# A sequence transform on 96-row runs, with both mirrors on partitions of their own, in a fused 2D-FFT and maxout kernel

## The chip, the cores and the metric

The kernel runs on one core of one Trainium2 chip. The metric is the time on the device in microseconds (us), the median of several runs. "Before" is the kernel as it stood, "after" the kernel with the change.

## What is computed

```python
X = np.fft.fft(x, axis=1)              # x: 8 x 3072 x 256, float32
X = np.fft.fft(X, axis=2).real         # over the sequence, then over the features
t = X.reshape(8 * 3072, 256)
h = np.maximum(np.maximum(t @ w1, t @ w2), t @ w3)      # w1, w2, w3: 256 x 768
out = h @ w_out                        # w_out: 768 x 256, out: 24576 x 256, float32
```

The matmuls run in bf16 with float32 sums. The transform over the features is a 256 x 256 matrix, so it is multiplied into w1, w2, w3 and w_out once, at the start; the tables and the products are made on the chip. What is left for each batch is the transform over the 3072 rows. x is real, so row 3072 - k of the result is row k with the mirror image of its features: the kernel computes the 1536 rows of one half (tE, the part even in k, and tO, the odd part) and forms both halves' hidden layers from them, with sums and differences of the same products.

## The kernel before

The kernel is written for a planner that keeps the order of the program: each engine gets its instructions in the order in which the Python code issues them, and waits are put in by data dependence. So the order of the lines is the order of each engine's queue, and a place in a queue is a decision of the author. A DMA is issued by an engine (SP, ACT or POOL) and takes a place in that engine's queue too.

**x comes in** as 24 x 128: row n = 128 a + bb, with `load_rows` (L100). A batch is cut into four chunks of 32 bb; each chunk is four DMAs, one for each group of 64 features, so that partition (group, a) holds rows of 64 float32, 256 bytes each. Later batches go through SP's queue into `xs` (four buffers); batch 0 is split over all three queues. `turn_chunk` (L118) is the POOL copy that casts a chunk to bf16 and turns it, so that for each feature `dl` the 128 bb lie side by side. It may be given an instruction that it has to follow ("folds first").

**Stage one**, `Mix.s` (L337, L339): 64 matmuls per batch, one for each `dl`, with x (96 x 128) as the loaded weights and `m24blk` (96 columns: 24-point cosines and sines for four feature groups) moving. Thirteen PSUM groups are evicted by ACT to `ub`.

**The folds**, `Mix.fold` (L350 to L373): DVE adds and subtracts features and their mirror images, from `ub` into `zE` and `zO`, in bf16, some in descending order.

**Stage two**, `Mix.k` (L387 to L399): 44 matmuls of 128 columns and 6 of 64, with zE or zO as weights and the tables `cos_t`, `sin_t`, `nsin_t` moving; ACT evicts the six groups to `tE` and `tO`. `end` does the one row in the middle of the half (`t_mid`, three matmuls of one column).

**The two layers.** A batch is three blocks of 512 rows, a block six groups `jc` of 128 hidden columns: 18 **units** a batch. A unit is `unit_plus` (L415, L416: four matmuls of 512 columns into `pse2` and `pse3`, which have two buffers each), `unit_out` for the rows k (ACT takes ReLU of one at L429, DVE the maximum with the other at L430: `hp`), then `finish` of the unit before: `unit_minus` (L423, two matmuls of 512 columns into the same PSUM, with `gD`, the difference to the rows 3072 - k) and a second `unit_out` (`hm`). Then `l2_some(10)` issues ten steps of the second layer of the block before: `l2_block`, four slots of 128 rows each with 12 matmuls of 256 columns (L439), the linear part (L455, L463), DVE's sum `ot` (L468), one direct store on SP (L483, rows k, 24 apart) and one indirect store on POOL (L473, rows 3072 - k). The maximum of three is taken as relu(difference) and max because w1's product is taken off the other two and given back by the linear part.

**The plan.** After a unit's second layer, pieces for the next batch are issued from a table, filled by `at(batch, unit, piece)` (L611): `s0` to `s12`, the folds `fA0` to `fC1`, `kE0` to `kO2`, `end` (lists `ahead`, `ahead0`, and the first unit `begin`, 5 from batch 2 on), the casts of the batch after that (each behind the last fold) and the loads of the one after. So the sequence transform of a batch is spread over the units of the batch before it.

**The start.** Before any unit, the tables (L215 to L232), batch 0's x, the weights (POOL's queue, both halves of w1, w2 and w3 early, L159 to L168), twelve matmuls without use for the clock (L565), stage one, the folds and kE0, kO0 of batch 0, and the products `gE`, `gO`, `gD` for the first half of the hidden columns (`product`, `keep_product`, L268, L280, L281; gD is POOL's). The second half (`prep_first`) and the second layer's product `gw` (`prep_second`) are placed by `prep_some`: the first of them ahead of the first unit.

**The end.** The last block's second layer is `l2_last` (L486): direct stores only, all on SP's queue but the first of the last slot, which is on ACT's (L519). The middle rows of all batches are done together in `l2_mid`.

Of the kernel before, what the change touches and what calls it, by code (L numbers as in the profile page):

```python
# [9 lines left out]
FP32 = mybir.dt.float32  # L10
# [9 lines left out]
def _reduce(nc, w, v, q, period, rnd, neg):  # L20

    shape = list(v.shape)
    for c in (rnd, neg):
        assert c.shape[0] == shape[0]
    wide = [shape[0], v.free_size()]
    nc.vector.scalar_tensor_tensor(out=q, in0=v, scalar=1.0 / period,
                                   in1=rnd.to_broadcast(wide), op0=ALU.mult, op1=ALU.add)
    nc.vector.scalar_tensor_tensor(out=q, in0=q, scalar=-ROUND,
                                   in1=neg.to_broadcast(wide), op0=ALU.add, op1=ALU.mult)
    nc.vector.tensor_tensor(out=w, in0=v, in1=q, op=ALU.add)  # L30


@with_exitstack
def kernel(
# [18 lines left out]

    DLS = ((20, 25), (25, 30), (30, 35), (35, 40), (40, 45),
           (15, 20), (45, 50), (10, 15), (50, 55),
           (5, 10), (55, 60), (60, 64), (0, 5))
# [7 lines left out]
    xs_pool = ctx.enter_context(tc.tile_pool(name="xs", bufs=4))  # L64
    x0_pool = ctx.enter_context(tc.tile_pool(name="x0", bufs=2))
    u_pool = ctx.enter_context(tc.tile_pool(name="ubuf", bufs=1))
    z_pool = ctx.enter_context(tc.tile_pool(name="zbuf", bufs=1))
    t_pool = ctx.enter_context(tc.tile_pool(name="tbuf", bufs=2))

    m24blk = consts.tile([96, 96], BF16, tag="m24blk")  # L70
# [4 lines left out]
    cos_t = consts.tile([128, 13 * 128], BF16, tag="cos_t")  # L75
    sin_t = consts.tile([128, 13 * 128], BF16, tag="sin_t")
    nsin_t = consts.tile([128, 13 * 128], BF16, tag="nsin_t")
# [14 lines left out]
    zO = consts.tile([128, 26 * 128], BF16, tag="zO")  # L92

    def x_rows(b):
        return x[b].rearrange("(a bb) (g dl) -> g a bb dl", bb=128, g=4)

    def load_rows(eng, dst, b, r0, r1, after=None):
        xr = x_rows(b)
        for g in range(4):
            ld = eng.dma_start(out=dst[g * 24:(g + 1) * 24], in_=xr[g, :, r0:r1, :])  # L100
            if after is not None:
                tc.add_manual_dep(ld.ins, after.ins.name, AFTER, reason="weights first")

    def load_chunk(b, ch, after=None):
        xs = xs_pool.tile([96, 32 * 64], FP32, name="xs", tag="xs")
        load_rows(nc.sync, xs.rearrange("p (bb dl) -> p bb dl", dl=64), b,
                  ch * 32, ch * 32 + 32, after)
        return xs

    raw = {}  # L110
    turned = {}

    def turn_chunk(b, ch, after=None):

        if ch == 0:
            x0 = x0_pool.tile([96, 64 * 128], BF16, name="x0", tag="x0")
            turned[b] = x0.rearrange("p (dl bb) -> p dl bb", bb=128)
        cast = nc.gpsimd.tensor_copy(turned[b][:, :, ch * 32:(ch + 1) * 32],  # L118
                                     raw.pop((b, ch)).rearrange("p (bb dl) -> p dl bb", dl=64))
        if after is not None:  # L120
            tc.add_manual_dep(cast.ins, after.ins.name, AFTER, reason="folds first")
# [10 lines left out]
    HEAD = 80  # L132
    staged = []
    for (r0, eng) in ((80, nc.sync), (96, nc.scalar), (112, nc.sync)):
        xs = xs_pool.tile([96, 32 * 64], FP32, name="xs", tag="xs")
        load_rows(eng, xs[:, 0:16 * 64].rearrange("p (bb dl) -> p bb dl", dl=64), 0, r0, r0 + 16)
        staged.append((r0, xs))
# [178 lines left out]
    class Mix:  # L316
# [25 lines left out]
        def fold(self, k, which):  # L342
# [10 lines left out]
            if k < 2:  # L353
                return
# [377 lines left out]
```

## Time and profile before

| what | value |
|---|---|
| median of 3 runs | 432.57 us (431.87 to 433.15) |
| span of the profiled execution | 431.8 us |
| mean granted clock of TensorE | 0.996 |
| PE busy | 404.8 us, 94% of the span |
| DVE, ACT, POOL busy | 307.7 us, 272.8 us, 238.0 us |
| moved by DMA | 51.58 MB in 127,333 packets, 109,233 of them under 512 bytes |
| SP's queue (q1, hardware) | 44.8% of 16 DMA engines' span |
| ACT's queue (q10, hardware) | 0.8% |
| POOL's queue (q0, software) | 17.8% |

The profile is one execution. PE is the matmul engine, PEld its weight loads (beside the matmuls), DVE the vector engine, ACT the scalar engine, POOL GpSimd, SP the queue that only issues DMAs. Busy is the time inside instructions, added up; "x" counts them. Matmuls overlap, so a busy PE says little of whether it is at its peak: for that the starts of matmuls one after the other have to be compared. A row of a timeline has the start, the length, the engine, line, operation, the tiles (out<-in), shapes, and how many were drawn together; brackets name what ended the wait ahead of it. In a row of a group, the numbers behind the bar are busy us, mean ns of one, idle us ahead of them and what ended it. A row of a source line has smallest, median and largest length in ns and the first and last time.

### The profile page before, as it was taken

To read this page: it belongs to the slowest core of one execution; us is meant where nothing else is said; L and a number is where in the kernel's file an instruction comes from. 1 tells how busy PE (TensorE), PEld (TensorE's weight loads), DVE (VectorE), ACT (ScalarE), POOL (GpSimd) and SP (SyncE) were. 2 spreads that over 40 slices of the span, in tenths; PEclk is the share of its full clock that TensorE was granted. 3 is DMA by queue.
4 is the path that set the end of the run, shared out by engine and by line. 5 is a ranking of instruction groups with operands and counts; after the bars stand their busy time and mean duration, and the time that the engine had idled before them with its cause. 6 is when DMAs were issued, how large, how long until landed. Compare 5 with 4: busy or idle time off the path is not lost.

```text
span 431.8 us, 9121 instructions
## 1 busy us (share of the span) xinstructions
PE 404.8 (94%) x3196; PEld 271.1 (63%) x3252; DVE 307.7 (71%) x611; ACT 272.8 (63%) x512; POOL 238.0 (55%) x256
## 2 busy tenths in 40 slices
PE   0499979999999999999999999999999999999996
PEld 0175656666666666666666666667666666666665
DVE  7766748856886769576876679576876679667673
ACT  3576557666866676657765676757765676754650
POOL 7546762598249823984279624984369623214320
PEclk9989999999999999999999999999999999999999
DMA  9999999559731969159761969158762222111213
GB/s 115 111 160 124 128 139 192 152 113 174 147 107 53 179 131 204 63 99 160 145 145 73 167 127 199 73 97 155 148 141 74 74 63 74 62 56 52 105 66 130
DMA packets 127333, 51.58 MB, mean 119 GB/s; under 512 B 109233, under 2 KB 124344, under 8 KB 127288
## 3 DMA queue, kind: packets, MB, share of 16 engines
q1 hardware_dynamic: 104936, 35.80, 44.8%
q0 software_dynamic: 20624, 14.68, 17.8%
q10 hardware_dynamic: 1728, 0.52, 0.8%
q8 instruction: 25, 0.41, 0.4%
q14 instruction: 20, 0.16, 0.2%
HBM read 28.31 MB, written 25.17 MB: 124 GB/s over the span
## 4 chain that ended last, share of the span: by engine, by line
PE 84%; DVE 5%; ACT 4%; issue 2%; DMA 2%; POOL 1%; SPq 1%; ACTq 0%; DVEq 0%; POOLq 0%
PE po L439 27%; PE pse L415 14%; PE pse L423 13%; PE pse L416 11%; PE ps L337 6%; PE po L463 4%; PE pl L455 2%; DMA xs<-in_x_dram 2%; DVE hm L430 1%; ACT stmp L429 1%; PE warm L565 1%; PE psg L268 1%; PE ps L394 1%; DVE ot L468 1%; POOL x L118 1%
## 5 line engine op out<-in xcount | busy, mean ns | idle before, releaser
L429 ACT ACTIVATE stmp<-pse 128x512 bf16<-128x512 f32 x288 | 167.6, 605 | 57.4 <-PE pse L416 45.5
L473 POOL DMA_INDIRECT out_dram<-ot,rows_m x92 | 101.8, 1107 | 160.5 <-DVE ot L468 144.0
L430 DVE TENSOR_TENSOR hp<-pse,stmp 128x512 bf16<-128x512 f32 x144 | 99.3, 689 | 98.9 <-ACT stmp L429 64.9
L118 POOL CAST x<-xs 96x2048 bf16<-96x2048 f32 x28 | 104.6, 3745 | 11.3 <-DMA xs<-in_x_dram 8.8
L415 PE MATMUL pse<-tE,gE 128*128 128x512 bf16 x280 | 106.1, 379 | 2.2
L430 DVE TENSOR_TENSOR hm<-pse,stmp 128x512 bf16<-128x512 f32 x144 | 98.6, 685 | 6.3 <-ACT stmp L429 6.0
L416 PE MATMUL pse<-tO,gO 128*128 128x512 bf16 x245 | 92.7, 379 | 0.5
L439 PE MATMUL po<-wout_bf,hp 128*128 128x256 bf16 x576 | 86.1, 273 | 0.1
L423 PE MATMUL pse<-tO,gD 128*128 128x512 bf16 x284 | 84.9, 379 | 0.6
L439 PE MATMUL po<-wout_bf,hm 128*128 128x256 bf16 x576 | 78.6, 273 | 0.0
L339 ACT CAST ub<-ps 128x480 bf16<-128x480 f32 (+1 forms) x102 | 51.7, 556 | 37.2 <-PE ps L337 37.2
L439 PEld LDWEIGHTS <-hp 128*128 128x128 bf16 x576 | 56.4, 98 | 26.1
L439 PEld LDWEIGHTS <-hm 128*128 128x128 bf16 x576 | 56.4, 98 | 16.3
L468 DVE TENSOR_TENSOR ot<-po,even 128x512 f32<-128x512 f32 x92 | 62.7, 682 | 0.0
L423 PEld LDWEIGHTS <-gD 128*128 128x128 bf16 x288 | 27.7, 98 | 32.5 <-POOL gD L281 0.5
L416 PEld LDWEIGHTS <-gO 128*128 128x128 bf16 x288 | 28.1, 98 | 19.8 <-issue 1.6
L415 PEld LDWEIGHTS <-gE 128*128 128x128 bf16 x288 | 28.0, 97 | 19.5 <-issue 0.8
L337 PE MATMUL ps<-m24blk,x 96*128 96x96 bf16 x512 | 33.3, 213 | 2.7 <-POOL x L118 1.7
L463 PE MATMUL po<-gw,tO 128*128 128x512 bf16 x91 | 34.5, 379 | 0.0
L337 PEld LDWEIGHTS <-x 96*128 96x128 bf16 x512 | 30.5, 111 | 5.0 <-POOL x L118 2.0
L399 ACT CAST tO<-ps 128x512 bf16<-128x512 f32 x24 | 14.1, 586 | 22.4 <-PE ps L396 14.0
L459 ACT COPY even<-pl 128x512 f32<-128x512 f32 x46 | 27.3, 593 | 0.1
(127 smaller groups left out, 309.1 us busy)
## 6 DMA issues: line engine op xcount, KB each, us to landing
xs<-in_x_dram SPq DMA_DIRECT2D x112, 192.0 KB
out_dram<-ot SPq DMA_DIRECT2D x90, 128.0 KB
out_dram<-ot,rows_m POOLq DMA_INDIRECT x92, 4.4
w_bf<-in_moe_w_dram POOLq DMA_DIRECT2D x6, 192.0 KB, 5.6
out_dram<-ot SPq DMA_DIRECT2D x17, 64.0 KB
xs<-in_x_dram SPq DMA_DIRECT2D x8, 96.0 KB
x<-in_x_dram POOLq DMA_DIRECT2D x8, 96.0 KB, 11.5
xs<-in_x_dram ACTq DMA_DIRECT2D x4, 96.0 KB
```

The lines of the kernel that those rows point to most:

```text
L118: cast = nc.gpsimd.tensor_copy(turned[b][:, :, ch * 32:(ch + 1) * 32], raw.pop((b, ch)).rearrange("p (bb dl) -> p dl bb", dl=64))
L337: nc.tensor.matmul(ps1[:, i * 96:(i + 1) * 96], x0[:, d0 + i, :], m24blk, start=True, stop=True)
L339: evict(out=self.ub[:, d0 * 96:d1 * 96].rearrange("p (c i) -> p c i", i=n), in_=ps1[:, 0:n * 96].rearrange("p (i c) -> p c i", c=96))
L415: nc.tensor.matmul(pse[:, 0:n], gE[i][:, js], te, start=True, stop=False)
L416: nc.tensor.matmul(pse[:, 0:n], gO[i][:, js], to, start=False, stop=True)
L423: nc.tensor.matmul(pse, gD[i][:, js], to, start=False, stop=True, skip_group_check=True)
L429: nc.scalar.activation(out=stmp[:, 0:n], in_=pses[0][:, 0:n], func=AX.Relu)
L430: nc.vector.tensor_tensor(out=dst, in0=src3, in1=stmp[:, 0:n], op=ALU.max)
L439: nc.tensor.matmul(po, hcols(jc), wout_bf[:, jc * 256:(jc + 1) * 256], start=False, stop=(jc == NJC - 1), skip_group_check=True)
L463: nc.tensor.matmul(po, to[:, cp], gw[:, 256:768], start=True, stop=True)
L468: nc.vector.tensor_tensor(out=ot.rearrange("p (h c) -> p h c", h=2), in0=po.rearrange("p (h c) -> p h c", h=2), in1=lin.unsqueeze(1).to_br ...
L473: stored(nc.gpsimd.indirect_dma_start(out, bass.IndirectOffsetOnAxis(ap=rows_m[0:128 - lo, b * 12 + slot: b * 12 + slot + 1], axis=0), ot[ ...
```

## The change

x is now read as 32 runs of 96 rows: row n = 96 a + s, s from 0 to 95. A partition of `xr` holds (feature half m, mirror h, a): 2 x 2 x 32 = 128. With h = 0 it has s = 0 to 48, with h = 1 the same features of rows 96 - s (`load_x`; the rows are read in descending order), each piece 128 features or 512 bytes long. x is read so that each row is fetched once. The turn to bf16 is in two halves: m = 0 in four pieces on POOL (`turn_low`), m = 1, with its features in descending order, in eight pieces on DVE (`turn_high`) and a small copy. The plan has no rule that a POOL piece follows a DVE instruction any more.

Stage one's matmul sums over all 128 partitions, so that it adds both the row's mirror image and the feature's at once: 64 matmuls of 64 columns (`tab1`) and a small one (`tabx`) for each batch; ACT evicts eight groups and a small one to `tb`. In place of the folds, `y` issues four DMAs on ACT's queue, from SBUF to SBUF (64 partitions, two pieces of 2,176 bytes each), which bring the two feature halves and cosine and sine parts together in `yb`; `j` (twice, on DVE, 128 x 2,176, bf16) brings them into the order in which stage two takes them as weights, `yc`. Stage two has one matmul where there were two: 30 of 96 columns, eight of 32 or fewer, and two of one column, with tables `te_tab` and `to_tab` of 1,537 columns.

The rows of a slot are now 32 apart, in two or three stretches (`_runs`): 25 direct stores a batch for 13. At the end two stores are on ACT's queue for one.

The plan: stage one in units 6 to 9 (9 to 12 in batch 0), `y` behind the last piece, `j` in units 11 and 12 (14 and 15), stage two in units 12 to 17. The loads of batch b are in units 0 to 6 of batch b - 2, its turns on POOL and DVE in units 9 to 16 of the same.

The start: ACT issues half of batch 0's loads (eight DMAs) ahead of its own work. The second half of w1, w2 and w3, w_out and batch 1's x wait for the last of the first `y`'s DMAs. Batch 0's turns are on POOL (one), ACT (three) and DVE (four and the small one). There are 24 matmuls for the clock.

```diff
+def _runs(slot):
+
+    g, sub = divmod(slot, 4)
+    q = 5 * g + 1
+    if sub == 0:
+        special = {0: [(0, 32, 0)], 1: [(0, 16, 1024), (16, 32, 16)], 2: [(0, 32, 528)]}[g]
+        return special + [(32, 128, q)]
+    if sub == 1:
+        return [(0, 96, q + 1), (96, 128, q + 2)]
+    if sub == 2:
+        return [(0, 64, q + 2 + 1024), (64, 128, q + 3)]
+    return [(0, 32, q + 3 + 2048), (32, 128, q + 4)]
...
-    def turn_chunk(b, ch, after=None):
...
-        cast = nc.gpsimd.tensor_copy(turned[b][:, :, ch * 32:(ch + 1) * 32],
-                                     raw.pop((b, ch)).rearrange("p (bb dl) -> p dl bb", dl=64))
-        if after is not None:
-            tc.add_manual_dep(cast.ins, after.ins.name, AFTER, reason="folds first")
+
+    def load_x(b, s0, s1, engs, after=None):
+
+        rows = x[b].rearrange("(a s) (m f) -> m a s f", s=96, m=2)
+        for m in range(2):
+            for h in range(2):
+                lo, hi = (s0, s1) if h == 0 else (max(s0, 1), min(s1, 48))
+                src = rows[m]
+                src = src[:, lo:hi, :] if h == 0 else src[:, 97 - hi:97 - lo, :][:, ::-1, :]
+                p0 = 64 * m + 32 * h
+                ld = engs[h].dma_start(out=xr[b % 2][p0:p0 + 32, lo:hi, :], in_=src)
+                if after is not None:
+                    tc.add_manual_dep(ld.ins, after.ins.name, AFTER, reason="others first")
+
+    def turn(b, s0, s1, m, fn, f0=0, f1=128):
+
+        src, dst = xr[b % 2], xt[b % 2]
+        if m == 0:
+            return fn(out=dst[0:64, f0:f1, s0:s1],
+                      in_=src[0:64, s0:s1, f0:f1].rearrange("p s f -> p f s"))
+        return fn(out=dst[64:128, 1:128, s0:s1],
+                  in_=src[64:128, s0:s1, 127:0:-1].rearrange("p s f -> p f s"))
+
+    def turn_first(b, fn):
+
+        return fn(out=xt[b % 2][64:128, 0, 0:NS], in_=xr[b % 2][64:128, :, 0])
...
+    FIRST = ((0, 16), (16, 30), (30, 41), (41, 49))
+    for c, (s0, s1) in enumerate(FIRST):
+        load_x(0, s0, s1, (nc.sync, nc.scalar))
...
+    _reduce(nc, ang_r, ang_r, ang_q, 32.0)
+    nc.scalar.activation(out=ang_q, in_=ang_r, func=AX.Sin, scale=float(2.0 * math.pi / 32.0))
+    nc.vector.tensor_copy(out=tab1[:, 0:32], in_=ang_q[:, 0:32])
+    scal(tab1[:, 32:64], ang_q[:, 0:32], sig, ALU.mult)
+    scal(tabx, ang_q[:, 2 * RI:4 * RI], sgm, ALU.mult)
...
+    scal(kvec, kvec, sidx, ALU.mult, phi, ALU.add)
+    _reduce(nc, kvec, kvec, q, 3072.0)
...
+    turn(0, *FIRST[0], 0, pool)
+    turn(0, *FIRST[0], 1, dve)
+    turn(0, *FIRST[1], 0, act)
+    turn(0, *FIRST[1], 1, dve)
+    nc.scalar.activation(out=te_tab, in_=kvec, func=AX.Sin, scale=step)
...
+    def load_w(jh, after=None):
...
+            if after is not None:
+                tc.add_manual_dep(ld.ins, after.ins.name, AFTER, reason="others first")
+        return ld
+
+    first_half = load_w(0)
+    turn(0, *FIRST[2], 0, act)
+    turn(0, *FIRST[2], 1, dve)
+    nc.scalar.activation(out=q, in_=kvec, func=AX.Abs)
+    turn(0, *FIRST[3], 0, act)
+    turn(0, *FIRST[3], 1, dve)
+    turn_first(0, dve)
...
-        def s(self, k, x0, pool=ps_f, evict=nc.scalar.copy):
...
+        def s(self, k, pool=ps_f, evict=nc.scalar.copy):
             ps1 = pool.tile([128, 512], FP32, name="ps1", tag="ps")
-            for i in range(n):
-                nc.tensor.matmul(ps1[:, i * 96:(i + 1) * 96], x0[:, d0 + i, :], m24blk,
+            for i in range(8):
+                f = 2 * (8 * k + i)
+                nc.tensor.matmul(ps1[:, i * 64:(i + 1) * 64], self.x[:, f:f + 2, :], tab1,
                                  start=True, stop=True)
...
-        def fold(self, k, which):
...
+            evict(out=tbv[:, :, 0:32, 8 * k:8 * k + 8],
+                  in_=ps1.rearrange("p (i e c) -> p e c i", e=2, c=32))
+            if k == 0:
+                psx = pool.tile([128, 512], FP32, name="psx", tag="ps")
+                nc.tensor.matmul(psx[:, 0:2 * RI], self.x[:, 0:2, :], tabx,
+                                 start=True, stop=True)
+                evict(out=tbv[0:64, 1, :, 0], in_=psx[0:64, 0:2 * RI])
+
+        def y(self):
+            for f in range(2):
+                for cs in range(2):
+                    last = nc.scalar.dma_start(out=ybv[cs * 64:cs * 64 + 64, f],
+                                               in_=tbv[f * 64:f * 64 + 64, :,
+                                                       cs * RI:(cs + 1) * RI, :])
+            return last
+
+        def j(self, e, copy=nc.vector.tensor_copy):
+            copy(out=ycv[:, e].rearrange("p r (f m) -> p r f m", f=2),
+                 in_=ybv[:, :, e].rearrange("p f r m -> p r f m"))
 
         def k(self, which, g):
 
-            er, orr = self.zEr, zOr
-            parts = [(r, r * 128, 128) for r in range(4 * g + 1, min(4 * g + 5, 12))]
-            if g == 2:
-                parts += [(0, 0, 64), (12, 12 * 128, 64)]
+            special = {0: [(0, 0, 32)], 1: [(0, 0, 16), (16, 16, 16)], 2: [(16, 0, 32)]}[g]
+            parts = special + [(5 * g + 1 + i, 32 + 96 * i, 96) for i in range(5)]
+            tab = (te_tab, to_tab)[which]
...
+            for (r, c0, wd) in parts:
+                nc.tensor.matmul(ps2[:, c0:c0 + wd], ycv[:, which, (r - 1) % RI, :],
+                                 tab[:, g * 512 + c0:g * 512 + c0 + wd], start=True, stop=True)
...
+            for (p0, p1, k0) in _runs(slot):
+                row = base + k0
+                stored(nc.sync.dma_start(out=out[row: row + 32 * (p1 - p0 - 1) + 1: 32, :],
                                          in_=ot[p0:p1, 0:256]), "direct", ("scattered",))
...
-                stored(eng.dma_start(out=out[row: row + 24 * (p1 - p0 - 1) + 1: 24, :],
+                eng = nc.scalar if sub == 2 and k < 2 else nc.sync
...
-    for _ in range(12):
-        nc.tensor.matmul(warm, cos_t[:, 1536:1664], cos_t[:, 1152:1664], start=True, stop=True)
+    for _ in range(24):
+        nc.tensor.matmul(warm, md_all[:, 0:128], md_all, start=True, stop=True)
...
+    for k in range(8):
+        m.s(k, pool=ps_s, evict=(act, dve)[k % 2])
+    y_first = m.y()
+    nc.scalar.activation(out=to_tab, in_=q, func=AX.Sin, scale=-step, bias=half_pi)
+
     for half in range(2):
-        keep_product(early[half], 0, half, 0, nc.scalar.copy)
+        keep_product(product(0, half, 0, ps_f, "ps"), 0, half, 0, dve)
     for half in range(2):
-        keep_product(product(1, half, 0, ps_s, "ps"), 1, half, 0, nc.scalar.copy)
+        keep_product(product(1, half, 0, ps_s, "ps"), 1, half, 0, dve)
+    for e in range(2):
+        m.j(e)
+    load_w(1, y_first)
+    wld = nc.gpsimd.dma_start(out=wout_bf.rearrange("p (jc c) -> p jc c", jc=NJC),
+                              in_=moe_w_out.rearrange("(jc p) c -> p jc c", jc=NJC))
+    for (s0, s1) in ((0, 13), (13, 25), (25, 37), (37, 49)):
+        load_x(1, s0, s1, (nc.sync, nc.sync), y_first)
...
+    CHUNKS = ((0, 13), (13, 25), (25, 37), (37, 49))
...
+    def turn_low(b, ch):
+        turn(b, *CHUNKS[ch], 0, pool)
+
+    def turn_high(b, k):
+        s0, s1 = CHUNKS[k // 2]
+        mid = s0 + 6
+        turn(b, *((s0, mid), (mid, s1))[k % 2], 1, dve)
+        if k == 7:
+            turn_first(b, dve)
...
-        at(0, (3, 5, 7, 9)[ch], lambda ch=ch: fetch(2, ch))
+        at(0, (3, 5, 6, 7)[ch], lambda ch=ch: turn_low(1, ch))
+        at(0, (8, 10, 12, 14)[ch], lambda ch=ch: fetch(2, ch))
+        at(1, (0, 1, 3, 4)[ch], lambda ch=ch: turn_low(2, ch))
+    for k in range(8):
+        at(0, (3, 4, 5, 5, 6, 6, 7, 8)[k], lambda k=k: turn_high(1, k))
+        at(0, (16, 17, 18, 19, 20, 21, 22, 23)[k], lambda k=k: turn_high(2, k))
+    for b in range(3, B):
+        for ch in range(4):
+            at(b - 2, (0, 2, 4, 6)[ch], lambda b=b, ch=ch: fetch(b, ch))
+            at(b - 2, (9, 11, 13, 15)[ch], lambda b=b, ch=ch: turn_low(b, ch))
+        for k in range(8):
+            at(b - 2, 9 + k, lambda b=b, k=k: turn_high(b, k))
+
+    ahead0 = {9: ("s0", "s1"), 10: ("s2", "s3"), 11: ("s4", "s5"), 12: ("s6", "s7", "y"),
+              14: ("j0",), 15: ("j1", "kE0", "kO0"), 16: ("kE1", "kO1"), 17: ("kE2", "kO2", "end")}
+    ahead = {6: ("s0", "s1"), 7: ("s2", "s3"), 8: ("s4", "s5"), 9: ("s6", "s7", "y"),
+             11: ("j0",), 12: ("j1", "kE0"), 13: ("kO0",), 14: ("kE1",), 15: ("kO1",), 16: ("kE2",),
+             17: ("kO2", "end")}
```

More of the change, by code (lines that the diff above doesn't have):

```diff
@@ L251 @@
     nc.scalar.activation(out=nmd_all, in_=vm, func=AX.Sin, scale=float(-2.0 * math.pi / 256.0))
[L252 to L260 removed]
+    phi = small("phi")
@@ L616, in piece @@
         if what[0] == "s":
[L617 to L619 removed]
+            mm.s(int(what[1:]))
+        elif what[0] == "y":
+            mm.y()
+        elif what[0] == "j":
+            mm.j(int(what[1]))
         elif what[0] == "k":
```

379 lines of the change are left out of this document (127 added, 252 removed).

## The prediction

> **What bounds the kernel now.** I read the page's busy line and chain first, then the table of stretches, one row for each of two whole batches (18 units of 6 long matmuls each; the marks are the same DVE row one batch apart).
>
> ```profile
> PE 404.8 (94%) x3196; PEld 271.1 (63%) x3252; DVE 307.7 (71%) x611; ACT 272.8 (63%) x512; POOL 238.0 (55%) x256
> PE 84%; DVE 5%; ACT 4%; issue 2%; DMA 2%; POOL 1%; SPq 1%; ACTq 0%; DVEq 0%; POOLq 0%
> ```
> ```profile
> core 0: us, PE busy (x) PEld busy (x) DVE busy (x) ACT busy (x) POOL busy (x), PEclk, DMA share, GB/s
> 175.58:223.97 48.39, 48.02 (x389) 32.40 (x394) 35.49 (x72) 32.52 (x63) 29.32 (x29) 1.00 0.66 132
> 320.75:369.14 48.39, 48.01 (x389) 32.44 (x394) 35.55 (x72) 32.52 (x63) 26.05 (x28) 1.00 0.20 67
> ```
> A batch takes 48.39 us at DMA shares of 0.66 and 0.20 alike, so **x loads cost nothing in the middle**: halving their packets can pay only at the start. A busy PE row says little, so I add up start-to-start distances from PE's timeline:
>
> ```profile
> 52.85 0.22 PE L394 MATMUL ps<-nsin_t,zO 128*128 128x128 bf16 x1
> 52.91 0.22 PE L396 MATMUL ps<-cos_t,zO 128*128 128x128 bf16 x1
> ...
> 53.18 0.19 PE L394 MATMUL ps<-nsin_t,zO 128*128 128x64 bf16 x1
> 53.21 0.19 PE L396 MATMUL ps<-cos_t,zO 128*128 128x64 bf16 x1
> ...
> 204.89 0.59 PE L337 MATMUL ps<-m24blk,x 96*128 96x96 bf16 x10
> 205.31 0.81 PE L415 MATMUL pse<-tE,gE 128*128 128x512 bf16 x2
> ```
> So 128 columns take 0.056 us, 64 take 0.030, 96 take 0.042 (0.42 over 10); 512 take 0.216, 256 take 0.109, in the same timeline. A batch: 108 x 0.216 = 23.3 (pse), 12 x 0.216 = 2.6 and 156 x 0.109 = 17.0 (po, pl), 64 x 0.044 = 2.8 (stage one; the last of each ten is a little wider), 44 x 0.056 + 6 x 0.030 + 3 x 0.027 = 2.7 (stage two). Sum 48.4 = the measured 48.39: **PE has no stall in a steady batch**, so what PE is spared comes off, unless ACT or DVE now makes it wait. A unit without extras is 6 x 0.216 + 10 x 0.109 = 2.38 us.
>
> **The change part by part.**
>
> *PE, steady.* Stage one: 65 matmuls of 64 or fewer columns, 65 x 0.030 = 1.95 for 2.8. Stage two: 30 of 96 columns and 10 of 32 or fewer, 30 x 0.042 + 10 x 0.027 = 1.55 for 2.7. Gain 2.0 per batch; batches 1 to 7: **-14.3**; batch 0's later stage two, inside units 2 to 7: **-0.8**. Widths and weight loads all have rows, so I hold this to 2 us.
>
> *ACT, y().* Thirteen evictions (0.56) become eight and a small one: free, ACT had room. But four DMAs now stand in ACT's queue at the end of unit 9, behind the eviction of s7, before unit 10's two ReLUs.
>
> ```profile
> 205.30 1.02 ACT L339 CAST ub<-ps 128x480 bf16<-128x480 f32 x2 [0.81 <-PE ps L337]
> 206.21 1.11 ACT L429 ACTIVATE stmp<-pse 128x512 bf16<-128x512 f32 x2
> ```
> ```profile
> L519 ACTq DMA_DIRECT2D out_dram<-ot x1: 385/385/385, 427.9 to 427.9; - x1
> L100 ACTq DMA_DIRECT2D xs<-in_x_dram x4: 310/456/626, 0.7 to 2.2; - x4
> ```
> An issue on ACT takes 0.31 to 0.63 us; each y DMA has 128 pieces like L519's, so 4 x 0.37 = 1.5. Take 205.31 as the end of s7: the evictions end at 206.3, the issues at 207.8, the two ReLUs at 208.4 and 209.0. The matmuls of unit 11 may overwrite the psum of unit 9 after the second ReLU; PE would be there at 205.31 + 2.38 = 207.7. It waits 1.3 us for ACT, some more for DVE's max. Bounds: 0.7 (issues at 0.31 and an earlier s7) to 2.0; I take 1.4, seven times: **+9.8**. Should an issue also wait for an older DMA on the same semaphore, that comes on top.
>
> *DVE: folds out, turns and j in.* The folds were some 6.6 us a batch. Added: eight turns of 64 partitions, 6,223 elements, and two joins j of 2,176.
>
> ```profile
> L235 DVE CAST x<-xs 96x1024 bf16<-96x1024 f32 x3 | 2.0, 683 | 2.1 <-DMA xs<-in_x_dram 2.1
> L118 POOL CAST x<-xs 96x2048 bf16<-96x2048 f32 x28 | 104.6, 3745 | 11.3 <-DMA xs<-in_x_dram 8.8
> ```
> L235 is the nearest row: 683 - 150 fixed = 0.52 ns an element, though its operands lie in order and the turns' do not; f32 rows with two inputs (L26, 1,092 ns for 896) give 1.04. At 0.52 the turns are 4.4 us, a j 1.28. Units 9 to 16: DVE 8 x 1.63 (hp, hm and two thirds of an ot at 0.61 each) + 4.4 + 2.6 = 20.0 against PE's 20.9. But in units 11 and 12 DVE has 1.63 + 0.55 + 1.28 = 3.5 against PE's 2.4 and 2.6, and PE is only one unit ahead: I take 0.8 us, six times: **+5**. At 1.04 DVE has 25.5 and PE loses 4 a batch (+24 in all); at best 0. The Trainium skill (VectorE: DVE Perf Modes, "The perf-mode tier table") has a bf16 copy within SBUF at four elements a cycle; by that a j would be some 0.7 us, the +5 nearly nothing, and no row here shows it.
>
> j0 also waits for y to land. Its 1.1 MB is issued by 207.8; indirect stores of 128 KB land 4.4 us after issue, loads of 192 KB in 5.6; DVE reaches j0 near 213. I count nothing; late, it would hold every max behind it.
>
> *POOL.* Four casts of 1,664 or 1,536 elements, at 3745 / 2048 ns, are 3.0 and 2.8 us: 11.5 for 15. Off the path. *SP.* 25 direct stores a batch for 13, at 0.38 us, but 16 loads of half the packets; SP has room. At the end two more stores, one issue each: **+0.4**.
>
> *The start.* Before, s(0) begins at 21.7, the first pse at 33.2, and PE waits 1.73 us for a cast at s(1):
>
> ```profile
> 21.69 3.31 PE L337 MATMUL ps<-m24blk,x 96*128 96x96 bf16 x35 [0.54 <-issue]
> 33.20 0.38 PE L415 MATMUL pse<-tE,gE 128*128 128x512 bf16 x1
> 60.04 0.60 PE L337 MATMUL ps<-m24blk,x 96*128 96x96 bf16 x10 [1.73 <-POOL x L118]
> ```
> ```profile
> w_bf<-in_moe_w_dram POOLq DMA_DIRECT2D x6, 192.0 KB, 5.6
> out_dram<-ot,rows_m POOLq DMA_INDIRECT x92, 4.4
> ```
> After: ACT issues eight x loads first, and the last waits for the fourth to land (1.9 MB: 9 to 12 us, bounded by the 115 GB/s of the page's early slices and about twice that for double packets). Only then comes the table load (1.28) and the sine for tab1: 11.4 to 14.2. DVE stands behind it with some 9.7 us of tables (three passes of 1,537 elements at 0.52 and one at 1.04 ns alone are 4.6): 21 to 24. ACT's te_tab, two turns and an Abs, 1.4 us each, follow, beside DVE's turns: s(0) at 28 (26 to 31). Matmuls and evictions 3, four issues 1.5, landing 4: y landed at 36.7. **load_w(1) waits for exactly this**, and PE's queue holds the product of those weights ahead of the first pse: two issues of 0.72, then 5.6, then 0.7: first pse at 43.7, 10.5 later (bounds 6 to 14). The 1.73 wait goes, since x(1) has 30 us until unit 9: **+9**. Without load_w's wait, y, two j and two evictions would still put it near 40.
>
> **Sum** on the profiled execution's 431.8 (the page gives its span alone; the runs' median is 0.8 above): 431.8 - 14.3 - 0.8 + 9.8 + 5 + 0.4 + 9 = 440.9, with 0.8: **441.7**.
>
> **Rivals.**
>
> *Faster.* ACT's issues and j fall into slack and the start costs +5: 432.6 - 15.1 + 0.4 + 5 + 3 = 426; with the start at +9 still 430. For it: ACT is 63% busy, DVE was full for 14 us of folds without stalling PE. Against: ReLUs are strictly behind the issues, and PE runs one unit ahead at most.
>
> *Slower still: DVE and POOL hinder each other.* Before, the casts carry a wait for the folds; now POOL's casts and DVE's turns stand in the same units 9 to 16. The one meeting of such work in the trace:
>
> ```profile
> L281 POOL TENSOR_SCALAR gD<-gO,dif x4: 1232/1268/1653, 30.9 to 42.7; 128x384 bf16<-128x384 bf16 x4
> 30.89 1.65 POOL L281 TENSOR_SCALAR gD<-gO,dif 128x384 bf16<-128x384 bf16 x1 [5.72 <-ACT gO L280]
> ```
> Beside folds it took 0.4 us more than the others, and a fold of 24 elements beside it took 0.57 us against 0.26. If the later one waits for the other's whole instruction: casts fill 11.5 of 21 us, so of ten DVE pieces 5.5 meet one and wait half of 2.9 each, 8 us; less the 2 us or so of slack, 6 a batch for five batches: +30; if half, +15. It decides from about 0.3 us a meeting, the slack in a unit. 456 to 472. The Trainium skill (SBUF — State Buffer, "Who interferes with whom") says just this: a DVE copy in a two-port mode and a GpSimd instruction exclude each other for the whole instruction. The fold that went on beside gD speaks for something milder, but it had another form.
>
> *The wider x rows do not matter.* Then the start alone loses what I gave them: +3, within the forecast.
>
> **How the numbers follow.** Forecast (434 to 455) 0.45; port rival (455 and up) 0.25; faster 0.25; within 0.3% (1.3 us, about what a measurement of this kernel tells from no change) 0.05. The range runs from 426 to 466, with about one in ten beyond each end.
>
> **What would show it.** PE distances of 0.030 and 0.042 us at the new stage lines; a PE wait for ACT in unit 11 of every batch, with ACTq DMA rows ahead of it; first pse near 44; j at 0.6, 1.3 or 2.4 us; DVE turns of one length (0.55 each) or spread up to 3 us (the port rival). The forecast is wrong if a steady batch is below 47.5 us or above 50, or the first pse comes before 39.

## The result and the profile after

The changed kernel takes 543.85 us (median of 4 runs, 542.98 to 545.9), the kernel before 432.79 us beside it: a ratio of 1.258, 95% interval 1.254 to 1.262. I had forecast 441.7, at most 466. The direction was right, the size was not: 111 us instead of 9.

The busy line and the chain of the page after:

```profile
PE 418.1 (77%) x3113; PEld 260.6 (48%) x3168; DVE 401.2 (74%) x542; ACT 268.1 (50%) x474; POOL 230.8 (43%) x246
PE 52%; DVE 19%; issue 11%; DMA 6%; ACT 4%; ACTq 4%; POOL 1%; DVEq 0%; SPq 0%
```

In the chain, issue is time in which the engine waited for nothing that the profile shows, and ACTq is ACT's queue while it issues DMAs. PE held 84% of the chain before and holds 52% now. DVE has 94 us more of busy time, though it lost its folds. Where the time went is a sum over batches. I take the first `hp` row of each batch as its mark:

| | first mark | batch 0 | 1 | 2 | 3 | 4 | 5 | 6 | last mark to end |
|---|---|---|---|---|---|---|---|---|---|
| before | 34.5 | 51.0 | 49.7 | 48.9 | 48.4 | 48.4 | 48.4 | 48.4 | 54.2 |
| after | 54.8 | 66.4 | 69.8 | 60.4 | 61.2 | 59.5 | 60.5 | 52.8 | 55.8 |

The differences are 20.3 for the start, 87.4 for the seven batches, 1.6 for the end: 109.3, the difference of the spans (541.2 - 431.8 = 109.4). So the start is a fifth of the loss. The batches are nearly all of the rest: 11 to 13 us in each of batches 2 to 5, 15 and 20 in batches 0 and 1, 4 in batch 6. Batch 1 holds six of batch 2's turns on DVE beside all of batch 3's, and DVE is busy for 61.4 of its 69.8 us. Two whole batches in the table of stretches (columns as in the prediction: stretch, length, busy of PE, PEld, DVE, ACT, POOL, granted clock, DMA share, GB/s):

```profile
251.38:312.60 61.22, 50.05 (x377) 31.21 (x382) 47.07 (x61) 31.90 (x59) 28.80 (x29) 0.94 0.48 122
312.60:372.10 59.50, 48.95 (x376) 31.00 (x382) 47.04 (x61) 31.85 (x59) 28.83 (x29) 0.97 0.49 126
```

No engine is full (DVE 47 of 60), the DMA engines are half idle, the clock is below 1. That is the look of engines that wait for one another. In the first of the two PE is idle for 10.8 us: 4.2 for ACT's ReLU, 5.8 for DVE, the rest for an eviction of stage one and a little more. PE's timeline in the batch from 251.4 shows for whom:

```profile
272.76 0.63 PE L339 MATMUL ps<-tab,xt 128*128 128x64 bf16 x16
...
282.85 0.58 PE L385 MATMUL pse<-tE,gE 128*128 128x512 bf16 x1 [4.22 <-ACT stmp L399]
283.23 0.63 PE L386 MATMUL pse<-tO,gO 128*128 128x512 bf16 x1
...
291.20 0.41 PE L368 MATMUL ps<-te_tab,yc 128*128 128x32 bf16 x6 [0.54 <-DVE yc L358]
...
292.99 0.38 PE L385 MATMUL pse<-tE,gE 128*128 128x512 bf16 x1 [0.95 <-DVE hm L400]
```

Sixteen stage one matmuls take 0.47 us up to the next start, 0.029 each: that step of the forecast is right. But PE stands 4.22 us for one ReLU of ACT, then runs at about 0.4 us a matmul of 512 columns (0.216 at full clock), and stands for DVE again and again. ACT's timeline at the same place:

```profile
276.05 1.07 ACT L341 CAST tb<-ps 128x512 bf16<-128x512 f32 x2 [0.31 <-PE ps L339]
277.15 4.46 ACTq L352 DMA_DIRECT2D yb<-tb  x4
281.71 1.09 ACT L399 ACTIVATE stmp<-pse 128x512 bf16<-128x512 f32 x2 [4.59 <-DMA yb<-tb]
```

The four issues of `y` take 4.46 us (0.60, 1.25, 0.63 and 1.86), where I had put 1.5. This is the longest `y` of the eight, the others take 2.8 to 3.9 us, and in batches 0 to 6 PE stands 2.6 to 4.2 us for the ReLU behind them. And DVE's turns have two lengths; its rows, and POOL's casts at the same times:

```profile
238.29 3.13 DVE L126 CAST xt<-xr 64x762 bf16<-64x762 f32 x1
...
243.37 1.01 DVE L126 CAST xt<-xr 64x762 bf16<-64x762 f32 x1
...
246.33 2.54 DVE L126 CAST xt<-xr 64x762 bf16<-64x762 f32 x1
...
289.86 1.28 DVE L358 COPY yc<-yb 128x2176 bf16<-128x2176 bf16 x1
```
```profile
237.83 2.87 POOL L124 CAST xt<-xr 64x1536 bf16<-64x1536 f32 x1
...
245.28 2.88 POOL L124 CAST xt<-xr 64x1536 bf16<-64x1536 f32 x1
```

POOL's casts end at 240.70 and 248.16, the two long turns at 241.42 and 248.87: 0.7 us behind, both. The turn that met no cast took 1.01. In every steady batch three of eight turns meet a cast (3.1, 3.1 and 2.5 us): 5.7 us of DVE's time in a batch.

At the start, PE, ACT and POOL, one fence each:

```profile
31.85 0.39 PE L339 MATMUL ps<-tab,xt 128*128 128x64 bf16 x8 [3.64 <-DVE xt L131]
...
51.49 0.82 PE L279 MATMUL psg<-w_bf,md_all 128*128 128x384 bf16 x2 [5.46 <-DMA w_bf<-in_moe_w_dram]
...
52.74 0.63 PE L385 MATMUL pse<-tE,gE 128*128 128x512 bf16 x1
```
```profile
0.74 12.33 ACTq L116 DMA_DIRECT2D xr<-in_x_dram  x8
13.16 1.28 ACT L202 ACT_TABLE_LOAD   x1 [13.16 <-DMA xr<-in_x_dram]
```
```profile
41.21 2.48 POOL L292 TENSOR_SCALAR gD<-gO,dif 128x384 bf16<-128x384 bf16 x2 [28.32 <-ACT gO L291]
43.64 2.21 POOL L253 DMA_DIRECT2D w_bf<-in_moe_w_dram  x3
```

The order is as forecast (ACT's issues, the sine, the tables, the turns, `y`, the weights, the first pse), each step later: the sine at 14.5 (11.4 to 14.2 forecast), s(0) at 31.85 (26 to 31), first pse at 52.7 (39.2 to 47.2). The weights are issued from 43.64 on, behind two `gD` that I had left out of POOL's queue, and the DMA that PE waits for lands 7 us after its issue.

### The profile page after: what moved, and what is told of

It is laid out like the page before. It is cut to its first block, busy times and chain, and to the rows that moved or that the text cites. A ratio compares the mean times of both kernels' runs of the same rounds, so it can differ in the third digit from the quotient of the medians.

```text
span 541.2 us, 9028 instructions
## 1 busy us (share of the span) xinstructions
PE 418.1 (77%) x3113; PEld 260.6 (48%) x3168; DVE 401.2 (74%) x542; ACT 268.1 (50%) x474; POOL 230.8 (43%) x246
## 4 chain that ended last, share of the span: by engine, by line
PE 52%; DVE 19%; issue 11%; DMA 6%; ACT 4%; ACTq 4%; POOL 1%; DVEq 0%; SPq 0%
PE po L409 16%; PE pse L385 11%; PE pse L393 10%; PE pse L386 8%; DVE hp L400 5%; DVE hm L400 5%; DVE xt L126 5%; ACTq L352 4%; PE ps L339 3%; DMA xr<-in_x_dram 2%; PE po L432 2%; ACT tb L341 2%; DMA yb<-tb 2%; DVE ot L437 2%; ACT stmp L399 2%
## 5 line engine op out<-in xcount | busy, mean ns | idle before, releaser
L442 POOL DMA_INDIRECT out_dram<-ot,rows_m x92 | 120.7, 1312 | 259.6 <-DVE ot L437 249.5
L385 PE MATMUL pse<-tE,gE 128*128 128x512 bf16 x285 | 112.1, 393 | 55.4 <-DVE hm L400 29.3
L126 DVE CAST xt<-xr 64x762 bf16<-64x762 f32 (+5 forms) x60 | 106.6, 1784 | 1.7
L386 PE MATMUL pse<-tO,gO 128*128 128x512 bf16 x251 | 100.0, 398 | 0.5 <-issue 0.4
L409 PE MATMUL po<-wout_bf,hp 128*128 128x256 bf16 x576 | 89.1, 279 | 1.9 <-issue 1.6
L124 POOL CAST xt<-xr 64x1536 bf16<-64x1536 f32 (+2 forms) x29 | 85.3, 2944 | 0.0
L409 PE MATMUL po<-wout_bf,hm 128*128 128x256 bf16 x576 | 82.6, 282 | 0.1
L341 ACT CAST tb<-ps 128x512 bf16<-128x512 f32 x60 | 33.0, 589 | 24.2 <-PE ps L339 14.8
L339 PE MATMUL ps<-tab,xt 128*128 128x64 bf16 x512 | 22.0, 197 | 12.3 <-DVE xt L131 7.7
L339 PEld LDWEIGHTS <-xt 128*128 128x128 bf16 x512 | 20.5, 101 | 14.5 <-issue 9.3
```

The costliest lines, as they stand in the source:

```text
L124: return fn(out=dst[0:64, f0:f1, s0:s1], in_=src[0:64, s0:s1, f0:f1].rearrange("p s f -> p f s"))
L126: return fn(out=dst[64:128, 1:128, s0:s1], in_=src[64:128, s0:s1, 127:0:-1].rearrange("p s f -> p f s"))
L339: nc.tensor.matmul(ps1[:, i * 64:(i + 1) * 64], self.x[:, f:f + 2, :], tab1, start=True, stop=True)
L341: evict(out=tbv[:, :, 0:32, 8 * k:8 * k + 8], in_=ps1.rearrange("p (i e c) -> p e c i", e=2, c=32))
L385: nc.tensor.matmul(pse[:, 0:n], gE[i][:, js], te, start=True, stop=False)
L386: nc.tensor.matmul(pse[:, 0:n], gO[i][:, js], to, start=False, stop=True)
```

## The experiments

The theories: (A) `y`'s issues on ACT and the half clock behind them are the loss; (B) the meetings of POOL's casts and DVE's turns are; (C) they lie in the same units and cover one another; (D) the start hangs on the second half of the weights. Where no interval stands with a time it is a single one; the kernel before took 431.0 to 432.6 us beside them, and the changed kernel's own four times lie 2.9 us apart.

**`y` on SP (e1).**

```diff
-                    last = nc.scalar.dma_start(out=ybv[cs * 64:cs * 64 + 64, f],
+                    last = nc.sync.dma_start(out=ybv[cs * 64:cs * 64 + 64, f],
```

> The four DMAs of y are issued by SP instead of ACT, at the same place of the plan. Theory A (y's issues on ACT cost the most: PE stands for 4.4 us in unit 11 and then runs at half the granted clock, 3.1 us more): no PE wait for ACT in unit 11, no half clock in a steady batch, 7.5 us off each of seven batches, 544 - 52 = 492; if DVE's turns then take back half of it, about 515. Rival (DVE is the bound, y only decides where PE waits): less than 10 us off, 534 or more. If y comes late from SP's queue, a wait of j for a DMA shows on DVE.

537.1 us. The wait for ACT is gone, and 7 us with it. In the same batch PE now stands 2.2 us for DVE's `hm` and 2.3 for DVE's `yc` (at most 1.7 and 0.5 in the changed kernel): one more turn, which met no cast before (1.1 us), now meets one and takes 2.8. Theory A alone falls.

**Casts and turns apart (e2).**

```diff
-            at(b - 2, (9, 11, 13, 15)[ch], lambda b=b, ch=ch: turn_low(b, ch))
+            at(b - 2, (17, 19, 20, 22)[ch], lambda b=b, ch=ch: turn_low(b, ch))
```

> For batches 3 to 7 POOL's four casts are moved out of the units of DVE's turns (9, 11, 13, 15) to units 17, 19, 20, 22, counted on into the next batch; batches 1 and 2 stay. Theory B (a turn that meets a POOL cast stands until the cast ends: in a steady batch three turns take 3.1, 3.1 and 2.5 us, the other five 1.0 to 1.1): all turns of those batches at 1.0, DVE 5.8 us a batch shorter, 5 x 5.8 = 29 off at most, 515 to 525. Rival (the long turns are long by themselves, by place or by DMA traffic): the lengths stay, 541 to 546.

524.9 us, the upper end of B's range. In the steady batches all turns are 1.0 to 1.1 us. The wait for ACT stays (3.6 to 4.2 us), and the edit brings one of its own: PE's stage one now stands 1.1 to 1.8 us a batch for the casts that were moved.

**Matmuls without use in the stall (e3).**

```diff
+    def filler():
+        psd = ps_f.tile([128, 512], FP32, name="psd", tag="ps")
+        for _ in range(20):
+            nc.tensor.matmul(psd, md_all[:, 0:128], md_all, start=True, stop=True)
+
+    for b in range(B - 1):
+        at(b, 10 if b else 13, filler)
```

> Twenty matmuls of 512 columns without use (20 x 0.216 = 4.3 us) are put behind unit 10 (13 in batch 0), where PE stands anyway while ACT issues y. Theory A's second half (the idle time itself brings the half clock): no half clock after y in the steady batches, unit 11 runs at 0.216 us a matmul, 3.1 us off each of seven batches, 522. Rival (the half clock comes from something else, or DVE would have held PE there in any case): 540 or more; if the fillers are not hidden, 544 + 7 x 4.3 = 574.

543.6 us: the fillers are hidden and unit 11 runs at 0.216 us a matmul, so PE's idle time does bring the half clock. But nothing is won: PE then stands 2.35 us for `yc`, and in most batches the half clock follows there. In batch 2 it does not (1.00 for 0.94), and the batch takes 60.6 us as before (60.4).

**The turn in another form (e4).**

```diff
+    def reduce_copy(out, in_):
+        return nc.vector.tensor_reduce(out=out, in_=in_.unsqueeze(3),
+                                       axis=mybir.AxisListType.X, op=ALU.max)
...
-        turn(b, *((s0, mid), (mid, s1))[k % 2], 1, dve)
+        turn(b, *((s0, mid), (mid, s1))[k % 2], 1, reduce_copy)
```

> DVE's turns in the plan are written as a maximum over an axis of length one (a tensor_reduce) instead of a copy: same elements, same places, same result; POOL's casts stay in the same units. Theory B1 (the meeting is one of the instruction's form: the copy takes something that POOL's cast holds): turns at about 0.95 to 1.0 us whether a cast runs beside them or not, 5.8 us a batch off DVE, up to 35 to 40 off in all, 505 to 515. Rival B2 (any DVE instruction that reads and writes SBUF waits for a POOL cast): three in eight stay at 2.5 to 3.1 us, 540 to 546. The Trainium skill (SBUF: State Buffer, Who interferes with whom) says that copy, cast and tensor_scalar can take the shared pair and tensor_reduce never does; no run here has shown it so far.

528.9 us. The source line's row (smallest, median, largest length in ns):

```profile
L613 DVE TENSOR_REDUCE xt<-xr x56: 1465/1498/1711, 65.3 to 414.2; 64x762 bf16<-64x762 f32 x49, 64x889 bf16<-64x889 f32 x7
```

All 56 have one length a size, with POOL's casts in the same units as ever (one from 288.62 to 291.48, a turn from 290.20 to 291.70 beside it). So the meeting is one of the instruction's form (B1): the copy waits, the reduction does not. The reduction takes 1.5 us instead of 1.0, so that eight of them give back 4 of the 5.7 us a batch; my 0.95 for it was wrong. The Trainium skill (SBUF — State Buffer, "Who interferes with whom") names copy and cast as instructions that can take a port pair shared with GpSimd, and tensor_reduce as one that never contends on this chip; these rows agree.

**Both, e1 and e2 (e5).** The two diffs together.

> Both edits: y on SP's queue and, for batches 3 to 7, POOL's casts out of the units of DVE's turns. Alone they gave 544 to 537 and to 525. Theory C (ACT's and DVE's delays lie in the same units and cover each other, so that each edit alone only shows the other): together far more than 7 + 19; a steady batch is PE's 46.4 plus 0.8 at stage one and some 2 us for DVE, about 49.5 for 60.8, five times, and 5 to 8 us in each of batches 1 and 2: 470 to 480. Rival (the gains only add up): 518. Rival (something else in the batch has a limit of its own, as SP's queue with y behind the stores): 490 to 510 with a DMA or SP named ahead of j.

531.6 us, worse than e2 alone, and C's number (470 to 480) is far off. Batches 2 to 5 are as long as in e2 (57.2 us on average, for 56.8), batches 0 and 6 are 3 to 4 us longer. DVE shows what is behind the two:

```profile
282.10 1.29 DVE L358 COPY yc<-yb 128x2176 bf16<-128x2176 bf16 x1 [3.73 <-DMA yb<-tb]
```

SP issues the four from 273.81 to 277.89, and they land only 4 us later; `j0`, placed two units behind `y`, holds every `hp` and `hm` behind it (it waits 3.0 to 3.8 us in batches 1 to 5, 7.0 and 5.5 in batches 0 and 6). From the first issue to `j0` it takes 7.5 to 8.3 us in batches 1 to 5. In e2 ACT's delay made that 10 us, in e1 the meetings 8.1 to 9.3, and `j0` waited in neither in these batches. So three delays lie one behind the other; the late casts of e2 are here too, with the same 1.1 to 1.8 us for PE.

**The weights early (e6).**

```diff
     first_half = load_w(0)
+    load_w(1)
+    wld = nc.gpsimd.dma_start(out=wout_bf.rearrange("p (jc c) -> p jc c", jc=NJC),
...
-    load_w(1, y_first)
-    wld = nc.gpsimd.dma_start(out=wout_bf.rearrange("p (jc c) -> p jc c", jc=NJC),
```

> Of the start alone: the second half of w1, w2, w3 and w_out is issued by POOL right behind the first half and waits for nothing; batch 1's x still waits for the first y. Theory D (PE's first pse stands behind the product of those weights, which POOL issues at 43.6, behind its two gD and y, and which land 7.0 us later): first pse at 46 to 47 for 52.7, where the last of kO0's eviction leaves it, and 5 to 6 off, 538. Rival (the weights now share the DMA engines with x, stage one of batch 0 comes later): s(0) at 33 to 35 for 31.85 and 0 to 3 off.

540.3 us; first pse at 47.4 (52.7), near D's forecast, s(0) at 31.6. Of these 5.3 us 3.6 are left at the end.

**The start (e7).** As e6, and:

```diff
-        load_x(0, s0, s1, (nc.sync, nc.scalar))
+        load_x(0, s0, s1, (nc.sync, nc.sync))
...
+    scal(kvec, kvec, sidx, ALU.mult, phi, ALU.add)
+    _reduce(nc, kvec, kvec, q, 3072.0)
...
     nc.scalar.activation(out=ang_q, in_=ang_r, func=AX.Sin, scale=float(2.0 * math.pi / 32.0))
...
-    scal(kvec, kvec, sidx, ALU.mult, phi, ALU.add)
-    _reduce(nc, kvec, kvec, q, 3072.0)
```

> The start alone, three edits: the weights as in the run before; all of batch 0's x loads on SP, so that ACT's table load and sine do not stand behind four DMAs that wait; DVE's four passes over 1,537 elements (4.8 us) ahead of the sine's results, where DVE has been idle from 10.9 to 14.75. Theory D: DVE's turns can begin when x has landed, s(0) at 26 to 28 for 31.85, first pse at 40 to 42 for 52.7, about 532. Rival (x itself lands late when one queue issues all of it): s(0) stays at 31 or later and the time is that of the run before.

538.9 us, s(0) still at 32.0, first pse at 48.0. DVE's turns end at 27.9 now, but ACT's three turns (7.9 us) and two table passes between them end at 31.9. Neither theory had named that one. In e9 below the three turns stand ahead of those passes, among other edits, and s(0) is at 26.0.

**A plan with time for each step (e8), the same with one thing put back (e10, e11), and with a new start (e9).** The core of e8, besides `y` on SP (and batch 1's turns on DVE in the form of e4, batch 2's loads and turns earlier, batch 0's list spread likewise):

```diff
-            at(b - 2, (9, 11, 13, 15)[ch], lambda b=b, ch=ch: turn_low(b, ch))
+            at(b - 2, (15, 17, 18, 20)[ch], lambda b=b, ch=ch: turn_low(b, ch))
...
-            at(b - 2, 9 + k, lambda b=b, k=k: turn_high(b, k))
+            at(b - 2, 5 + k, lambda b=b, k=k: turn_high(b, k))
...
-    ahead = {6: ("s0", "s1"), 7: ("s2", "s3"), 8: ("s4", "s5"), 9: ("s6", "s7", "y"),
-             11: ("j0",), 12: ("j1", "kE0"), 13: ("kO0",), 14: ("kE1",), 15: ("kO1",), 16: ("kE2",),
-             17: ("kO2", "end")}
+    ahead = {5: ("s0",), 6: ("s1", "s2"), 7: ("s3", "s4"), 8: ("s5", "s6"), 9: ("s7", "y"),
+             13: ("j0",), 14: ("j1",), 15: ("kE0",), 16: ("kO0",), 17: ("kE1", "end"),
+             18: ("kO1",), 19: ("kE2",), 20: ("kO2",)}
```

e10 has the casts at `(5, 7, 9, 11)[ch]`, beside the turns again; e11 has `nc.scalar.dma_start` in `y` again. e9 takes the early weights and the loads on SP from e7; on ACT the three turns come ahead of `md_all`, and DVE's passes for `te_tab`, with `te_tab` itself, behind stage one.

> In the run with both edits j0 then stood 3.7 us for y's DMAs to land. Here, besides y on SP, the whole plan gives every step its time: stage one in units 5 to 9, j0 and j1 four and five units behind y (13, 14), stage two in units 15 to 20 (into the next batch), DVE's turns in units 5 to 12, POOL's casts in 15, 17, 18, 20; batch 1's DVE turns as tensor_reduce, batch 2 loaded earlier; the start as it is. Theory C' (three delays in a row, turns that meet casts, ACT's or SP's issues, y's landing, each covered by the next): with all three out of the way a steady batch is 46.4 to 47.5 us, the time 544 - 6 x 13 = 460 to 470 (first pse still at 52.7, batch 0 slow). Rival (the pieces have a limit that spreading cannot take away, DVE's 8 turns and 2 j's, 11 us a batch, above all): a steady batch of 52 or more, 490 to 510.

> The new plan with one thing put back: POOL's casts of batches 3 to 7 in units 5, 7, 9, 11, beside DVE's turns. If a meeting costs DVE what it did (2.1 us each, two to four a batch) and nothing else hides it: 3 to 6 us a batch above the run with the plan alone, five times, 15 to 30. If DVE's slack takes it up: under 5.

> The new plan with one thing put back: y issued by ACT. If the four issues cost what PE stood for in the changed kernel (4.4 us and 3.1 us of half clock): 7.5 us in each of seven batches, 52 above the run with the plan alone. My prediction had 1.4 each, 10 in all. If only the issue time counts and the clock holds: 15 to 30.

470.3, 513.3 and 510.0 us. A steady batch of each, in this order:

```profile
216.90:265.80 48.90, 47.20 (x383) 30.35 (x382) 41.68 (x60) 30.92 (x59) 28.39 (x29) 1.00 0.64 153
```
```profile
233.30:291.70 58.40, 48.80 (x384) 30.87 (x382) 50.75 (x61) 31.24 (x59) 27.48 (x28) 0.97 0.52 128
```
```profile
236.00:290.50 54.50, 48.85 (x383) 31.04 (x382) 41.73 (x60) 30.90 (x59) 28.37 (x29) 0.97 0.55 138
```

Here two of the three stand alone; `y`'s landing was not put back by itself. The meetings (four a batch) make DVE's busy time 9.1 us longer (41.68 to 50.75) and the batch 9.5: all of it arrives, none of the slack that I had counted on takes it up. The time of e10, 43 us above e8, is far over the 15 to 30 that I had expected. `y` on ACT makes the batch 5.6 us longer with DVE's busy time unchanged, less than the 7.5 expected, about 40 us in seven batches. With both away and `y` given time, 12 us a batch are gone, and 74 of the 111 us.

> The new plan and a new start: batch 0's x on SP alone, weights early, ACT's three turns ahead of its other tables, DVE's table passes for te_tab behind stage one, POOL's memsets behind its first cast. s(0) at 24 to 26 for 31.85, first pse at 38 to 41 for 52.7, so 12 to 14 below the run with the plan alone: with a steady batch of 47 this is 39 + (432 - 33) - 14 = 424, and a little for batch 0: 425 to 435, against 432 before the change. If the plan alone stays at 490 or more, 480 and no version here beats the old kernel.

459.7 us, 1.063 of the kernel before (1.057 to 1.069). First pse at 40.9, as forecast; the time is 25 us over the range. Two things make that up: batch 0 stays at 62.8 us (51.0 before), and the steady batches are 48.8 to 48.9, so that none of the 14 us that the forecast took off for PE arrives.

**The fillers again, with nothing behind them (e12).** e11 with the piece of e3, `range(15)` for `range(20)`.

> The new plan with y issued by ACT, as in the run at 510, and fifteen matmuls of 512 columns without use (15 x 0.216 = 3.2 us) behind unit 10 (13 in batch 0), where PE stands 3.4 us for ACT. In the first filler run another stall followed and the clock fell there instead; here nothing else stalls PE for long. Theory (idle time brings the half clock): no half clock in batches 2 to 6 and 1.5 to 2.9 us off each batch, 498 to 502. Rival (the half clock has another cause, or the time after it was not lost): 507 to 513.

510.8 us, against 510.0. The stretch of one batch:

```profile
238.00:292.70 54.70, 50.66 (x399) 31.86 (x397) 41.70 (x61) 30.96 (x59) 28.42 (x29) 1.00 0.55 137
```

The clock is 1.00 and the batch as long as with 0.97. PE arrives earlier and stands 2.88 us for DVE's `hm` a little later, 1.71 in e11. So the half clock comes from the idle time, and cost nothing here: what `y` on ACT costs is then the backlog of ReLUs and of DVE's maxima behind it, for which PE waits whatever its clock.

**Once more at the rest (e13).** From e9 (besides, batch 1's casts and one cast of each later batch are moved by one or two units, `j1` goes to unit 15, and batch 0's stage one goes back to units 9 to 12):

```diff
-        load_x(1, s0, s1, (nc.sync, nc.sync), y_first)
+        load_x(1, s0, s1, (nc.sync, nc.sync))
...
-        at(0, (3, 4, 5, 5, 6, 6, 7, 8)[k], lambda k=k: turn_high(1, k, reduce_copy))
+        at(0, (1, 2, 3, 4, 5, 6, 7, 8)[k], lambda k=k: turn_high(1, k, reduce_copy))
...
-            at(b - 2, 5 + k, lambda b=b, k=k: turn_high(b, k))
+            at(b - 2, (4, 5, 6, 7, 8, 9, 12, 14)[k], lambda b=b, k=k: turn_high(b, k))
```

> The version at 459.7 with its three visible remainders worked on: batch 1's x does not wait for the first y (batch 0 took 62.8 us for 48.9 of the others, with PE standing 4.7 us for batch 1's x), its turns spread one to a unit, and in the steady batches three of DVE's turns moved from the units that held PE for 0.56 us each. If these are what is left: 5 to 9 off in batch 0 and 1 to 1.5 in each of six batches, 443 to 449, still above the 432 of before, because the first pse stays at 41 (33.2 before). If batch 0 is bound by DVE's own work (eight turns of 1.5 us beside the second layer's weights): 452 to 458.

454.4 us, 1.050 of the kernel before (1.045 to 1.055), between the two forecasts. Its steady batches are 48.1 to 49.1 us, the old ones 48.4 to 48.9. Left are the start (first mark at 43.0 for 34.5), batches 0 and 1 (56.8 and 53.2 for 51.0 and 49.7) and 2.2 us behind the last mark. No version here beats the kernel before.

## Why the prediction was wrong, step by step

- **PE, steady and batch 0 (-14.3, -0.8)**: right as a sum of matmuls (0.029 us a matmul of 64 columns), but a gain only where nothing else stands in the way. Even e8 is at 48.90: in four units a batch PE stands 0.40 to 0.44 us for DVE's `hm` (0.56 counted from start to start), and its 2 us are gone.
- **ACT, `y` (+9.8)**: the step that failed first. The row that I took the issue from (0.37 us, a store of 128 pieces) was the wrong neighbour: `y`'s issues cost 0.60 to 1.86 us, on SP much as on ACT (in e5 603 ns at least, median 674, up to 1,591). What a batch then loses is 5.6 us (e11 against e8), four times the 1.4, and outside its bounds of 0.7 to 2.0. Why some issues take twice as long as others is not settled.
- **DVE (+5)**: `j` was right to the digit (1.28), by luck in part: its rate came from L235, a cast from float32, and `j` copies bf16. The unmet turn is 1.0 us for 762 elements, so the upper row (1.04 ns an element) was the near one, not L235, which has its operands in order. I had counted 24 for that row and taken 5.
- **"j0 also waits for y to land ... I count nothing"**: it was nothing only as long as ACT or the meetings came first; e5 shows 3.0 to 3.8 us in batches 1 to 5.
- **The rival "DVE and POOL hinder each other" (0.25)** was the right mechanism, with a price of one meeting near the measured one (half of 2.9 us; 1.5 to 2.1 in a steady batch of the changed kernel, up to 3.7 in e10). It was no alternative to the forecast, as I had it, but came on top of it: in the sum the meetings stood at nothing, and that is the second step that failed. I had let 2 us of slack take up part of it; e10 shows 9.5 us for 9.1.
- **The start (+9)** was 20.3. The order was right. s(0) came 3.9 us later than I had put it, with the turns of batch 0 longer than I had them (ACT's last two took 2.6 and 1.9 us for 1.4 each, DVE's four 7.3 together); `y` landed another 2.3 later (its issues again), the two `gD` ahead of the weights were not in the sum and held their issue 0.8 us past that landing, and the weights took 7.0 us to land for 5.6.
- **The sum** failed as a form. I priced each edit against slack as if the others were not there, and added. In this plan the three delays lie in the same units, and with one or two of them out PE waits for the next, or for what the edit itself made late (537, 525, 532); with all three out the time is 470. In the steady batch e1 gave back 2.2 us and e2 3.6, on the average of batches 2 to 5. What is taken away in full is 11.5 us, from 60.4 to e8's 48.9. The prices come near it: 5.7 for the meetings (3.1, 3.1 and 2.5 against 1.0 each, at the rate of e10, where DVE's time arrives whole) and 5.6 for `y` are 11.3. That is an estimate, since no run puts both back into e8's plan, and how much of it each has in the changed kernel stays open. The 35 us of batches 0 and 1 are taken apart by no run.
- **The half clock** is in the trace (0.94), and is a result, not a cause: without it a batch was as long (60.6 us for 60.4 in e3, 54.7 for 54.5 in e12).

## What to carry to other kernels

Work that is moved from one busy engine to three less busy ones has to be priced as a chain: its latency from the first step to the last, and each engine's queue behind each step, before any engine's total. When several delays lie in the same stretch, undoing one of them says little of its price; build a version in which none binds, then put them back one at a time.

## What the runs showed of the hardware

- A turn on DVE (a cast of 762 elements, out of SBUF and into it) that meets a POOL cast ends 0.7 us after the cast (0.66 to 0.72 in the 21 meetings of the changed kernel), whatever was left of the cast when the turn came; the reduction of e4 and the maxima from PSUM (0.68 to 0.69 us beside casts and without) do not wait.
- The issue of an indirect store on POOL holds a turn too. In e8 one turn of a steady batch comes 2.1 us into such an issue and ends 0.6 us behind it; in e10 the same turn finds a cast right behind the issue and stands through both. First e8, then e10, POOL and DVE:

```profile
236.89 3.18 POOL L442 DMA_INDIRECT out_dram<-ot,rows_m  x1 [3.60 <-DVE ot L437]
...
238.98 1.73 DVE L126 CAST xt<-xr 64x762 bf16<-64x762 f32 x1
```
```profile
255.19 3.18 POOL L442 DMA_INDIRECT out_dram<-ot,rows_m  x1 [3.22 <-DVE ot L437]
...
257.29 4.67 DVE L126 CAST xt<-xr 64x762 bf16<-64x762 f32 x1
...
258.41 2.84 POOL L124 CAST xt<-xr 64x1536 bf16<-64x1536 f32 x1
```

- It holds for tiny instructions too. At the start two DVE passes over 68 elements take 2.92 and 3.53 us, and end just behind the last of POOL's memsets (at 7.00) and its cast (10.56); the same operation over 512 elements takes 0.42:

```profile
4.13 2.92 DVE L22 TENSOR_SCALAR ang_q<-ang_r 128x68 f32<-128x68 f32 x1
7.09 3.53 DVE L24 TENSOR_SCALAR ang_q<-ang_q 128x68 f32<-128x68 f32 x1
```
```profile
3.38 3.37 POOL L237 MEMSET xt<- 128x1920 bf16 x2
6.65 0.35 POOL L238 MEMSET tb<- 128x256 bf16 x1
6.91 3.65 POOL L124 CAST xt<-xr 64x2048 bf16<-64x2048 f32 x1
```

- The page that I had set against the trace for `j` (VectorE: DVE Perf Modes, "The perf-mode tier table", in the Trainium skill) would have given, as an estimate, some 0.7 us by its four elements a cycle; the measurement decides, 1.28 us for 2,176 elements in runs of 64.
- PE's waits for ACT behind `y`, 2.6 to 4.2 us long, each go with 3.4 or 6.8 us at half the granted clock in the changed kernel, beginning within 1.5 us of the wait's end. Shorter idle times are not all alike: 2.35 us in e3 brought it in four batches of five, 2.5 to 3.0 us in three batches of e12 did not.
